# Loading the first rows of a in one transfer with a third row a head, in a fused state-space and feed-forward kernel

## The chip, the cores and the metric

The kernel runs on one core of a Trainium2 chip. A core has TensorE (PE, matrix products), VectorE (DVE), ScalarE (ACT), GpSimd (POOL) and SyncE (SP), which here only issues DMAs; each takes its own instructions in order, and semaphores tie them together. Data lie in SBUF and PSUM, both of 128 partitions, and come from DRAM by DMA over 16 DMA engines. The metric is the device time of one execution in microseconds, lower is better.

## The reference

Two blocks one after the other, all in float32. The first is a state-space scan over 4 batches and 8 heads of 768 steps, with inputs x (32 wide), B and C (16 wide) and a decay `a` per head and step:

```python
log_a = np.log(np.clip(a, 1e-06, 1.0))
for c in range(nc):                     # chunks
    cum = np.cumsum(la, axis=-1)
    L = np.exp(cum[:, :, :, None] - cum[:, :, None, :]) * causal
    y_intra = einsum('bhij,bhjd->bhid', einsum('bhin,bhjn->bhij', Cc, Bc) * L, xc)
    y_inter = einsum('bhin,bhnd->bhid', Cc, state) * np.exp(cum)[..., None]
    y[:, :, sl] = y_intra + y_inter
    state = decay_full * state + sum_j(Bc x_c * exp(cum_end - cum_j))
```

The second takes y as 3072 tokens of 256 and computes `g = h * sigmoid(1.702 h)` with `h = y @ w_in` (256 x 2048), and then `g @ w_out` (2048 x 256). The result does not depend on the chunk length; the kernel uses chunks of 64.

## The kernel before

**Tiling.** The 3072 tokens are six groups of 512 (`TG`). A group is two *pairs* of 256 steps, a pair is two blocks of 128, and a block is two chunks of 64. Batch 0 has 768 steps, so it is pairs 0, 1 and 2; pairs 0 and 1 make group 0, and pair 3 is the first of batch 1. For each group the state-space block gives `yT` (256 x 512, features on the partitions), `hidden` multiplies it with 16 tiles of w_in (`h`, two passes of 512 columns each, then Silu on ScalarE), and a second product goes through w_out. In later groups these products are done in a Strassen-like form (L934, L944, L1039).

**The order of work.** It is written out by hand, and `in_order` (L21) makes every engine follow the program text. So an instruction that waits holds back all that stands behind it on its engine. Hooks such as `at(in_hidden[0], k, ...)` put work behind the k-th tile of `hidden` of group 0.

**The start.** Everything that group 0 needs hangs on the first 512 steps of `a` of batch 0. They come in as `az0`, 128 x 256: four copies (one for each quarter of the partitions) of 32 rows, and in each copy row 2h + c holds half c of head h. Four DMAs load them, two from SP and two from ScalarE's queue (L278). Then: VectorE clips `az0` (L342), ScalarE takes the logarithm (L344), VectorE sums it up within chunks (`cum`, L346). TensorE fills PSUM banks with the causal mask (L530) and adds cum_i - cum_j for all heads of pairs 0 and 1 (`ab`, L536, picked out of the rows by the 0/1 operand `pick0`), ScalarE takes the exponential (L557): these are the decays L. `fold_ident(0)` (L336) builds an operand for later scans; it stands on VectorE ahead of the clip.

B and C of group 0 are loaded in blocks of 32 and transposed by VectorE (`turn_first`). C is then masked by head parity into `CT`, for pair 0 and for pair 1 by GpSimd (`mask_first`, L632). TensorE turns B back (L609), computes the scores `cb` of pair 0 (L664), then `rows` (the decay since the group's start, L515, exponential on ScalarE at L520 as `since`), then the scores of pair 1. VectorE multiplies scores and L (`weigh`, L675), TensorE computes the chunks' gains `A` (L695), ScalarE and VectorE sum them to states (L712, L717), and `finish` forms y from an `intra` (L818) and an `inter` part (L804). TensorE has fillers in between, products of ones that nobody reads: `keep_busy`, `pads` and `dense`.

**Pair 2.** Its rows of `a`, the last third of batch 0, are loaded apart, by GpSimd into `az1`, clipped by VectorE, and copied by ScalarE under a mask (`pick1`) into `X` (`pick_a`); TensorE spreads X over partitions by `fan` (L418), between the `intra` parts of pairs 0 and 1, and the decays of pair 2 are scanned from that much later.

**The weights.** They are float64 values handed over as pairs of 32-bit words, and the kernel makes float32 of them in ten pieces: 0 to 3 are two tiles of w_in each, 4 and 5 four tiles each, 6 to 9 are w_out. `fetch(i)` loads piece i with two DMAs from SP (L181); `fields` (L193, L196, VectorE) cuts out exponent and mantissa, `clamp` (L204, L205, ScalarE) moves the exponent, `rounded` (L209) and `join` (L223, L229, both VectorE) assemble the number in `w_in`. `narrow(i)` is rounded, join and the next piece's fields in an order that depends on i; for pieces 0 to 3 a join of all columns is two instructions, in two parts four smaller ones. The order about w_in's first pieces is:

```python
    fetch(1, held=nc.gpsimd)
    for i in range(2, 6):
        fetch(i)
...
    for i, k, c in ((2, 1, 1), (3, 2, 2), (4, 4, 7), (5, 8, 10), (6, 10, 14), (7, 14, 15)):
        at(in_hidden[0], k, lambda i=i: narrow(i))
        at(in_hidden[0], c, lambda i=i: clamp(i + 1))
```

`held` puts a memset by GpSimd (L172) ahead of piece 1's DMAs, into their target; it stands on GpSimd behind `since_start(0)` (`CsT`, L649), which needs `since`. SP, in order, therefore issues pieces 1 to 5 and all behind them only then. Other SP loads that come up: `az` (all of a), `spread_rows` (`af`, L272: rows of a read with each row repeated for 16 partitions), and `a<-scratch` (L262).

Of the kernel before, what the change touches and what calls it, by code (L numbers as in the profile page):

```python
# [16 lines left out]
P = 128  # L17
TG = 512
# [17 lines left out]
def kernel(  # L36
# [71 lines left out]
    az0 = ffn.tile([P, TG // 2], FP32, tag="b", name="az0").rearrange("p (c s) -> p c s", c=2)  # L108
    az1 = const.tile([P, NC - CG, P], FP32, name="az1")
    cum = const.tile([P, 2, P], FP32, name="cum")  # L110
# [104 lines left out]

    def join(i, parts=1):

        name, f, n = PIECES[i]
        n //= parts
        low, m, p2 = bits.pop(i)[1], mantissa.pop(i), power.pop(i)  # L220
        for k in range(parts):
            cols, fs = slice(k * n * DM, (k + 1) * n * DM), slice(f + k * n, f + (k + 1) * n)
            nc.vector.scalar_tensor_tensor(out=p2[:, cols], in0=low[:, cols], scalar=0x80000000,  # L223
                                           in1=p2[:, cols], op0=ALU.bitwise_and, op1=ALU.bitwise_or)
            if name == "in":
                dst, h = w_in[:, fs].rearrange("p f k e -> p (f k e)").unsqueeze(1), 1
            else:
                dst, h = w_out[:, :, fs].rearrange("p c f e -> p c (f e)"), 2
            nc.vector.scalar_tensor_tensor(  # L229
                out=dst, in0=m[:, cols].bitcast(FP32).rearrange("p (h e) -> p h e", h=h),  # L230
                scalar=2.0 ** -20, in1=p2[:, cols].bitcast(FP32).rearrange("p (h e) -> p h e", h=h),
                op0=ALU.mult, op1=ALU.mult)
        for n in NEXT.get(i, ()):
            fetch(n)

    def narrow(i):
        rounded(i)
        if i in (2, 4, 5, 6):
            join(i, 2 if i in (4, 5) else 1)
        if i == 6:  # L240
            decay_rows(0)
        if i + 1 < len(PIECES):
            fields(i + 1)
        if i not in (2, 4, 5, 6):
            join(i, 2 if i == 3 else 1)

# [29 lines left out]

    for r in range(R):
        (nc.sync, nc.scalar)[r % 2].dma_start(  # L278
            out=az0[32 * r:32 * r + 32].rearrange("p k s -> p (k s)"),
            in_=a[:2, :, :TG].rearrange("b h (c s) -> (b h) c s", c=PG))  # L280
    early = const.tile([P, 1], FP32, name="early")
# [29 lines left out]

    pick0 = picker("pick0", PG, PG, 1)

# [20 lines left out]
    def fold_ident(k, engine=nc.vector):  # L334
# [5 lines left out]

    fold_ident(0)
    nc.vector.tensor_scalar(out=az0, in0=az0, scalar1=1e-6, scalar2=1.0, op0=ALU.max,  # L342
# [4 lines left out]
        out=cum.rearrange("p k s -> p (k s)"), data0=carry.rearrange("p k s -> p (k s)"),  # L347
        data1=cum.rearrange("p k s -> p (k s)"), initial=0.0, op0=ALU.mult, op1=ALU.add)

    fans, flat = {}, {}  # L350
# [6 lines left out]

    def pick_a(p):

        assert divmod(2 * p, NC) == (0, CG)  # L360
        X = ffn.tile([P, 2, DM], FP32, tag="ob", name=f"X{p}")
        X = fans[p] = X.rearrange("p k (q i) -> p k q i", q=Q)
        for q in range(Q):
            nc.scalar.activation(X[:, :, q], az1, AF.Copy, scale=pick1[:, q:q + 1])


    APART = P // NH
    nc.gpsimd.memset(az1, 1.0)
    nc.gpsimd.dma_start(
        out=az1.rearrange("(h e) c s -> h e (c s)", e=APART)[:, 0], in_=a[0, :, TG:])  # L370

# [10 lines left out]
    for n in range(PG):  # L382
        t = whose[32 * n:32 * n + 32, n:n + 1]
        nc.gpsimd.affine_select(out=t, in_=t, pattern=[[-1, 1], [-PG, NH], [0, N]],
                                compare_op=ALU.is_equal, fill=0.0, base=-n,
                                channel_multiplier=1)
# [6 lines left out]
        out=part, in_=same[:, :, 0].rearrange("p (r q) -> p q r", q=Q), op=ALU.add, axis=AX.X)  # L393
    pick1 = const.tile([P, Q], FP32, name="pick1")
    nc.vector.tensor_reduce(
        out=pick1, in_=ident.rearrange("p (r q e) -> p q r e", q=Q, e=APART)[:, :, :, 0],
        op=ALU.add, axis=AX.X)

# [24 lines left out]
    def fan_all(p):  # L423

        ab = area(f"ab{p}")[:, :, :2 * Q * H]
        for r in range(R):
            fan(p, r, ab[:, r])
        fans[p] = ab

    def decay_fanned(p):  # L430
# [78 lines left out]
    def since_first():  # L509

        since[0] = ssd.tile([P, NC, P], FP32, tag="since", name="since0")
        rows = [bank(f"rows{p}")[:, :2 * P] for p in range(PG)]
        for p in range(PG):
            at = slice(32 * p, 32 * p + 32)
            nc.tensor.matmul(out=rows[p],  # L515
                             lhsT=whose[at, p].rearrange("p h n -> p (h n)"),
                             rhs=cum[at].rearrange("p k s -> p (k s)"), start=True, stop=True,
                             tile_position=(32 * p, 0), skip_group_check=True)
        for p in range(PG):
            nc.scalar.activation(since[0][:, 2 * p:2 * p + 2].rearrange("p c s -> p (c s)"),  # L520
                                 rows[p], AF.Exp)

    def drops():
# [42 lines left out]
    def area(name):  # L566
        return psa.tile([P, R, 4 * P], FP32, tag="cb", name=name)

    def turn_only(p, steps=range(3)):
# [14 lines left out]
        if 1 in steps:  # L584
            s["tp"] = s.pop("both")[:, 1]
            s["CT"] = ssd.tile([P, 2, Q, P], FP32, tag="CT", name=f"CT{p}")
            for q in range(Q):
                copy(s["CT"][:, :, q], s["tp"], part[:, q:q + 1])
        if 2 in steps and p < PG:
            tp = s["tp"]  # L590
            s["tp"] = ssd.tile([P, 2, P], FP32, tag="CsT", name=f"C{p}", bufs=3)
            copy(s["tp"], tp)
# [33 lines left out]
    def mask_first(p):  # L626

        s = st[p]
        s["CT"] = ssd.tile([P, 2, Q, P], FP32, tag="CT", name=f"CT{p}")
        if p:  # L630
            nc.vector.memset(s["CT"][:, 0, 0, :1], 0.0)
        nc.gpsimd.tensor_tensor(  # L632
# [137 lines left out]
    def finish(pairs, steps=range(2)):  # L770
# [39 lines left out]
        def intra(n, p):  # L810
            L = Ls[p]
            for k in range(2):
                for h in range(NH):
                    for i, side in enumerate(SIDES):
# [54 lines left out]
    def hidden(g, f):  # L869
# [3 lines left out]
        h = bank(f"h{g}_{f}")  # L873
        n = 2 if g == 0 and f in range(10, 13) else 1
        for k in range(NK):
# [277 lines left out]

    keep_busy(4, 0)
    both = area("ab0")
# [5 lines left out]
    turn_first("B")  # L1161
    clip(az1)
    differ_of(0)
# [5 lines left out]
    fields(0)  # L1169
    mask_first(1)  # L1170
    pick_a(PG)
    to = area("cb0")
    pads(9, to[:, 0])
    turn_back()
    ends_first(0)
    ends_first(1)
    rounded(0)
    score(range(PG), since_first, to)
    weigh(0)
# [260 lines left out]
```

## Time and profile before

| | us |
|---|---|
| three timed runs | 347.11, 347.58, 348.89 (median 347.58) |
| profiled execution, its own time | 347.67 |
| its span | 345.9 |
| TensorE busy | 339.2 (98%) |
| VectorE busy | 256.1 (74%) |
| ScalarE busy | 155.1 (45%) |
| GpSimd busy | 16.7 (5%) |

The profile is one execution. All times within it are counted from the start of the span; the span is a little shorter than the device time. A line such as `27.28 0.69 DVE p L193` reads: at 27.28 us, for 0.69 us, VectorE ran an instruction of line 193 that writes `p`. An `x96` behind it counts several instructions taken together, `SPq` is a DMA being issued on SP, `DMA` the transfer itself, `PEld` TensorE's loading of weights. The granted clock of TensorE is given in parts of full speed; it is full in every slice of this profile.

### The profile page before, as it was taken

The numbers are of one execution on the slowest core, as the hardware profiler recorded it, in microseconds if no ns is written. First come the engines' busy times: TensorE is split into PE (matmuls) and PEld (weight loads), VectorE is DVE, ScalarE is ACT, GpSimd is POOL, SyncE is SP. The second block draws the span as 40 slices with busy tenths as digits, with TensorE's granted clock in tenths as the row PEclk, the third lists the DMA queues.
The fourth block names the chain that finished last, engine by engine and source line by source line (L and its number), as shares of the span: only waits on it lengthen the run. The fifth ranks groups of instructions, "written<-read, shape, count | busy, mean of one in ns | idle before, by whom it ended". The sixth has DMA issues, their size and how long they took to land.

```text
span 345.9 us, 8116 instructions
## 1 busy us (share of the span) xinstructions
PE 339.2 (98%) x3380; PEld 270.2 (78%) x3380; DVE 256.1 (74%) x484; ACT 155.1 (45%) x352; POOL 16.7 (5%) x40
## 2 busy tenths in 40 slices
PE   8999999999999999999999999999999999999996
PEld 6633744555788888888888888888888888899996
DVE  5988999999799998858995667787564654465463
ACT  5786771507454324754332554442454322554320
POOL 7300110300000100000000000000000000000000
PEclk9999999999999999999999999999999999999999
DMA  6698899545637100435603036400000300000401
GB/s 160 132 289 211 217 239 133 152 67 102 122 63 127 36 0 15 65 99 100 110 27 51 2 78 121 64 0 3 0 4 2 62 2 0 0 2 0 63 0 62
DMA packets 90004, 25.76 MB, mean 74 GB/s; under 512 B 73416, under 2 KB 87248, under 8 KB 89968
## 3 DMA queue, kind: packets, MB, share of 16 engines
q1 hardware_dynamic: 89104, 24.72, 35.0%
q10 hardware_dynamic: 832, 0.52, 0.5%
q8 instruction: 26, 0.43, 0.5%
q14 instruction: 10, 0.08, 0.1%
q0 software_dynamic: 32, 0.01, 0.0%
HBM read 22.00 MB, written 3.24 MB: 73 GB/s over the span
## 4 chain that ended last, share of the span: by engine, by line
PE 92%; DMA 3%; SPq 2%; DVE 1%; issue 0%; ACT 0%; POOL 0%; DVEq 0%
PE acc L1039 28%; PE X L934 19%; PE Y L944 14%; PE o L976 8%; PE acc L1046 7%; PE h L878 7%; DMA bits<-in_moe_w_in_dram 3%; PE y L818 2%; PE cb L664 2%; SPq L181 1%; PE y L804 1%; PE A L695 1%; PE ab L536 1%; DMA az<-in_a_dram 1%; POOL CsT L649 0%
## 5 line engine op out<-in xcount | busy, mean ns | idle before, releaser
L939 ACT ACTIVATE ac<-X 128x256 f32<-128x256 f32 x76 | 29.1, 383 | 81.7 <-PE X L934 81.0
L1039 PE MATMUL acc<-mg,mw 128*128 128x256 f32 x192 | 54.5, 379 | 0.0
L1066 DVE TENSOR_TENSOR gT<-Y,ac 128x512 f32<-128x512 f32 x38 | 26.2, 689 | 38.1 <-PE Y L944 32.5
L911 ACT ACTIVATE gT<-gT 128x512 f32<-128x512 f32 (+1 forms) x76 | 38.9, 519 | 29.3 <-DVE gT L1066 28.8
L934 PE MATMUL X<-my,mi 128*128 128x256 f32 x152 | 45.2, 380 | 0.0
L1039 PEld LDWEIGHTS acc<-mg,mw 128*128 128x128 f32 x192 | 36.6, 190 | 4.9
L1066 DVE TENSOR_TENSOR gT<-Y,b 128x256 f32<-128x256 f32 x38 | 15.8, 419 | 28.5 <-PE Y L944 28.5
L878 PE MATMUL h<-yT,w_in 128*128 128x512 f32 (+1 forms) x92 | 35.5, 541 | 1.4 <-DVE w_in L229 0.9
L1039 PE MATMUL acc<-gT,w_out 128*128 128x256 f32 x128 | 35.5, 380 | 0.0
L878 PEld LDWEIGHTS h<-yT,w_in 128*128 128x128 f32 x92 | 17.2, 190 | 18.2 <-issue 12.8
L934 PEld LDWEIGHTS X<-my,mi 128*128 128x128 f32 x152 | 28.0, 190 | 4.0 <-ACT ac L939 0.3
L976 PE MATMUL o<-gT,w_out 128*128 128x512 f32 x64 | 28.3, 596 | 0.0
L902 DVE TENSOR_TENSOR mg<-gT 128x512 f32<-128x512 f32 x40 | 27.2, 681 | 0.0
L1039 PEld LDWEIGHTS acc<-gT,w_out 128*128 128x128 f32 x128 | 24.3, 190 | 3.4 <-ACT yT L853 0.2
L939 ACT ACTIVATE b<-X 128x256 f32<-128x256 f32 x38 | 14.6, 383 | 20.8 <-PE X L934 20.3
L934 PE MATMUL X<-yT,w_in 128*128 128x256 f32 x76 | 23.2, 389 | 0.0
L944 PE MATMUL Y<-yT,w_in 128*128 128x256 f32 x76 | 22.7, 381 | 0.0
L944 PE MATMUL Y<-my,mi 128*128 128x256 f32 x76 | 22.7, 381 | 0.0
L934 PE MATMUL X<-my,w_in 128*128 128x256 f32 x76 | 22.5, 380 | 0.0
L944 PE MATMUL Y<-yT,mi 128*128 128x256 f32 x76 | 22.5, 380 | 0.0
L976 PEld LDWEIGHTS o<-gT,w_out 128*128 128x128 f32 x64 | 11.9, 190 | 13.6 <-issue 12.7
L408 DVE TENSOR_TENSOR_SCAN L<-a,idents 128x1024 f32<-128x1024 f32 x9 | 20.5, 2279 | 0.3 <-DMA a<-scratch 0.3
(152 smaller groups left out, 547.8 us busy)
## 6 DMA issues: line engine op xcount, KB each, us to landing
a<-scratch SPq DMA_DIRECT2D x18, 256.0 KB, 4.9
bits<-in_moe_w_out_dram SPq DMA_DIRECT2D x8, 512.0 KB, 7.4
x<-in_x_dram SPq DMA_DIRECT2D x24, 128.0 KB, 3.7
out_dram<-ob SPq DMA_DIRECT2D x40, 64.0 KB, 2.0
bits<-in_moe_w_in_dram SPq DMA_DIRECT2D x8, 256.0 KB, 3.7
bits<-in_moe_w_in_dram SPq DMA_DIRECT2D x4, 512.0 KB, 11.4
b<-in_B_dram SPq DMA_DIRECT2D x20, 64.0 KB, 3.3
af<-in_a_dram SPq DMA_DIRECT2D x3, 384.0 KB
```

The costliest lines, as they stand in the source:

```text
L408: nc.vector.tensor_tensor_scan(out=L, data0=ra[p].rearrange("p k e -> p (k e)"), data1=idents.rearrange("p h i -> p (h i)"), initial=0.0, ...
L664: nc.tensor.matmul(out=s["cb"][side, r, k].rearrange("p (q i) -> p q i", q=Q), lhsT=BT[rows, k, side], rhs=CT[rows, k, :, side], start=Tru ...
L878: nc.tensor.matmul(out=h[:, cols], lhsT=w_in[:, f, k], rhs=yT[g][:, k, cols], start=(k == 0 and c == 0), stop=(k == NK - 1), skip_group_ch ...
L902: nc.vector.tensor_tensor(out=t[:, 0:2], in0=B[:, :, 1], in1=B[:, 0], op=ALU.subtract)
L911: nc.scalar.activation(o, i, AF.Silu, scale=GELU_SCALE)
L934: nc.tensor.matmul(out=s["X"], lhsT=lhsT, rhs=rhs, start=i == "1", stop=i == "4", skip_group_check=True)
L939: nc.scalar.activation(copy, s["X"], AF.Copy)
L944: nc.tensor.matmul(out=o, lhsT=lhsT, rhs=rhs, start=s.pop("new", False), stop=i != "5", skip_group_check=True)
L976: nc.tensor.matmul(out=o[c], lhsT=w_out[:, c, f], rhs=gT[g, f // 2][:, f % 2], start=(f == 0), stop=(f == NF - 1), skip_group_check=True)
L1039: nc.tensor.matmul(out=acc[g][0][i][:, cols], lhsT=w, rhs=h[:, cols], start=(j == 0 and k == 0 and (i, 0) in begins), stop=(j == NF // 2 - ...
L1046: nc.tensor.matmul(out=o[k] if type(o) is list else o[:, cols], lhsT=h[:, cols], rhs=w, start=(j == 0 and (i, k) in begins), stop=(j == NF ...
L1066: nc.vector.tensor_tensor(out=o, in0=v, in1=w, op=ALU.add)
```

## The change

`az0` now holds, in each of its four copies, 32 rows that run through the array as it lies: row 3h + c is the c-th 256 steps of head h, so that pair 2's rows (c = 2) are there too. One DMA on SP loads it, its source read four times over. `pick0` and `whose` step by 3 rows a head (NR), and `third` takes pick1's place. Beyond that:

- `az1`, its memset, its DMA on GpSimd and its clip go; `pick_a` makes X from the clipped `az0` with two multiplications and a memset on VectorE.
- CT of pair 1 is masked by ScalarE (`mask_blocks`), not by GpSimd.
- `fold_ident(0)` stands behind the scan to `cum`, `fold_ident(1)` in `narrow(6)`.
- Fillers: `keep_busy` 3 for 4, `pads` 6 for 9, `dense` 4 blocks of 64 columns for 8, into the free half of a `rows` bank.
- `intra` of group 0 runs by heads, then blocks, rather than by blocks, then heads.
- Joins: piece 1 in two parts; the first half of piece 3 ahead of piece 4's `fields`, the second behind; `clamp(4)` one tile later; tile 9 of `hidden` in two passes of half the columns for each weight.
- `turn_only` copies C's transpose out of PSUM for pair 3 as well (its condition was p < 2, which no call met).

```diff
-    def join(i, parts=1):
+    def join(i, parts=1, only=None):
...
-        for k in range(parts):
+        for k in range(parts) if only is None else only:
...
     def narrow(i):
         rounded(i)
         if i in (2, 4, 5, 6):
+            if i == 6:
+                fold_ident(1)
             join(i, 2 if i in (4, 5) else 1)
         if i == 6:
             decay_rows(0)
+        if i == 3:
+            join(i, 2, (0,))
         if i + 1 < len(PIECES):
             fields(i + 1)
-        if i not in (2, 4, 5, 6):
-            join(i, 2 if i == 3 else 1)
+        if i == 3:
+            join(i, 2, (1,))
+        elif i not in (2, 4, 5, 6):
+            join(i)
...
-    for r in range(R):
-        (nc.sync, nc.scalar)[r % 2].dma_start(
-            out=az0[32 * r:32 * r + 32].rearrange("p k s -> p (k s)"),
-            in_=a[:2, :, :TG].rearrange("b h (c s) -> (b h) c s", c=PG))
+    NR = S // (2 * P)
+    assert NH * NR <= 32 <= BH * NR
+    nc.sync.dma_start(
+        out=az0.rearrange("p k s -> p (k s)"),
+        in_=a.rearrange("b h (c s) -> (b h c) s", c=NR)[:32].unsqueeze(0).to_broadcast(
+            [R, 32, 2 * P]))
...
-    pick0 = picker("pick0", PG, PG, 1)
+    pick0 = picker("pick0", PG, NR, 1)
...
-    fold_ident(0)
     nc.vector.tensor_scalar(out=az0, in0=az0, scalar1=1e-6, scalar2=1.0, op0=ALU.max,
                             op1=ALU.min)
...
+    fold_ident(0)
...
-    def pick_a(p):
-
-        assert divmod(2 * p, NC) == (0, CG)
-        X = ffn.tile([P, 2, DM], FP32, tag="ob", name=f"X{p}")
-        X = fans[p] = X.rearrange("p k (q i) -> p k q i", q=Q)
+    def pick_a():
+
+        X = ffn.tile([P, 2, DM], FP32, tag="ob", name="X")
+        X = fans[PG] = X.rearrange("p k (q i) -> p k q i", q=Q)
         for q in range(Q):
-            nc.scalar.activation(X[:, :, q], az1, AF.Copy, scale=pick1[:, q:q + 1])
-
-
-    APART = P // NH
-    nc.gpsimd.memset(az1, 1.0)
-    nc.gpsimd.dma_start(
-        out=az1.rearrange("(h e) c s -> h e (c s)", e=APART)[:, 0], in_=a[0, :, TG:])
+            nc.vector.tensor_scalar(out=X[:, :, q], in0=az0, scalar1=third[:, q:q + 1],
+                                    scalar2=None, op0=ALU.mult)
+        nc.vector.memset(X.rearrange("p k q (s i) -> p k q s i", s=2)[:, :, :, :, 0], 0.0)
...
-    pick1 = const.tile([P, Q], FP32, name="pick1")
-    nc.vector.tensor_reduce(
-        out=pick1, in_=ident.rearrange("p (r q e) -> p q r e", q=Q, e=APART)[:, :, :, 0],
-        op=ALU.add, axis=AX.X)
+    third = const.tile([P, Q], FP32, name="third")
+    for q in range(Q):
+        at = NR * q + PG
+        nc.vector.tensor_reduce(
+            out=third[:, q:q + 1], in_=ident[:, at:at + 3 * (32 + NR * Q) + 1:32 + NR * Q],
+            op=ALU.add, axis=AX.X)
...
-        if 2 in steps and p < PG:
+        if 2 in steps and p == PG + 1:
             tp = s["tp"]
             s["tp"] = ssd.tile([P, 2, P], FP32, tag="CsT", name=f"C{p}", bufs=3)
             copy(s["tp"], tp)
...
         s["CT"] = ssd.tile([P, 2, Q, P], FP32, tag="CT", name=f"CT{p}")
-        if p:
-            nc.vector.memset(s["CT"][:, 0, 0, :1], 0.0)
         nc.gpsimd.tensor_tensor(
...
         def intra(n, p):
             L = Ls[p]
-            for k in range(2):
-                for h in range(NH):
+            for h, k in [(h, k) for h in range(NH) for k in range(2)] if early else [
+                    (h, k) for k in range(2) for h in range(NH)]:
                     for i, side in enumerate(SIDES):
...
-        n = 2 if g == 0 and f in range(10, 13) else 1
+        n = 2 if g == 0 and f in range(9, 13) else 1
...
-    keep_busy(4, 0)
+    keep_busy(3, 0)
...
     turn_first("C")
     turn_first("B")
-    clip(az1)
+    pick_a()
     differ_of(0)
...
     fields(0)
-    mask_first(1)
-    pick_a(PG)
+    mask_blocks(1)
     to = area("cb0")
-    pads(9, to[:, 0])
+    pads(6, to[:, 0])
     turn_back()
     ends_first(0)
     ends_first(1)
     rounded(0)
-    score(range(PG), since_first, to)
+    free = []
+    score(range(PG), lambda: free.append(since_first()), to)
...
-    dense(8, bank("dense"))
+    dense(4, free[0])
     finish(range(PG))
     join(0, 2)
-    fold_ident(1)
     fields(1)
     clamp(1)
     table(AF.Silu)
     rounded(1)
-    join(1)
+    join(1, 2)
     fields(2)
...
-    for i, k, c in ((2, 1, 1), (3, 2, 2), (4, 4, 7), (5, 8, 10), (6, 10, 14), (7, 14, 15)):
+    for i, k, c in ((2, 1, 1), (3, 2, 3), (4, 4, 7), (5, 8, 10), (6, 10, 14), (7, 14, 15)):
         at(in_hidden[0], k, lambda i=i: narrow(i))
         at(in_hidden[0], c, lambda i=i: clamp(i + 1))
```

More of the change, by code (lines that the diff above doesn't have):

```diff
@@ L108 @@
     az0 = ffn.tile([P, TG // 2], FP32, tag="b", name="az0").rearrange("p (c s) -> p c s", c=2)
-    az1 = const.tile([P, NC - CG, P], FP32, name="az1")
     cum = const.tile([P, 2, P], FP32, name="cum")
@@ L214 @@
     NEXT = {1: (6,), 5: (9,)}
-    def join(i, parts=1):
+    def join(i, parts=1, only=None):
         name, f, n = PIECES[i]
         n //= parts
-        low, m, p2 = bits.pop(i)[1], mantissa.pop(i), power.pop(i)
-        for k in range(parts):
+        low, m, p2 = bits[i][1], mantissa[i], power[i]
+        for k in range(parts) if only is None else only:
             cols, fs = slice(k * n * DM, (k + 1) * n * DM), slice(f + k * n, f + (k + 1) * n)
@@ L232, in join @@
                 op0=ALU.mult, op1=ALU.mult)
-        for n in NEXT.get(i, ()):
-            fetch(n)
+        if only is None or parts - 1 in only:
+            for t in bits, mantissa, power:
+                t.pop(i)
+            for n in NEXT.get(i, ()):
+                fetch(n)
     def narrow(i):
@@ L356, in clip @@
         nc.vector.memset(t.rearrange(by_chunk, s=2)[:, :, :, 0], 0.0)
-    def pick_a(p):
-        assert divmod(2 * p, NC) == (0, CG)
-        X = ffn.tile([P, 2, DM], FP32, tag="ob", name=f"X{p}")
-        X = fans[p] = X.rearrange("p k (q i) -> p k q i", q=Q)
-        for q in range(Q):
-            nc.scalar.activation(X[:, :, q], az1, AF.Copy, scale=pick1[:, q:q + 1])
-    APART = P // NH
-    nc.gpsimd.memset(az1, 1.0)
-    nc.gpsimd.dma_start(
-        out=az1.rearrange("(h e) c s -> h e (c s)", e=APART)[:, 0], in_=a[0, :, TG:])
+    assert divmod(2 * PG, NC) == (0, CG) and NC - CG == 2
+    assert DM == Q * P
+    def pick_a():
+        X = ffn.tile([P, 2, DM], FP32, tag="ob", name="X")
+        X = fans[PG] = X.rearrange("p k (q i) -> p k q i", q=Q)
+        for q in range(Q):
+            nc.vector.tensor_scalar(out=X[:, :, q], in0=az0, scalar1=third[:, q:q + 1],
+                                    scalar2=None, op0=ALU.mult)
+        nc.vector.memset(X.rearrange("p k q (s i) -> p k q s i", s=2)[:, :, :, :, 0], 0.0)
     same = ssd.tile([P, NH, D], FP32, tag="BT", name="same")
@@ L383 @@
         t = whose[32 * n:32 * n + 32, n:n + 1]
-        nc.gpsimd.affine_select(out=t, in_=t, pattern=[[-1, 1], [-PG, NH], [0, N]],
+        nc.gpsimd.affine_select(out=t, in_=t, pattern=[[-1, 1], [-NR, NH], [0, N]],
                                 compare_op=ALU.is_equal, fill=0.0, base=-n,
@@ L423, in fan_all @@
     def fan_all(p):
-        ab = area(f"ab{p}")[:, :, :2 * Q * H]
+        whole = area(f"ab{p}")
+        ab = whole[:, :, :2 * Q * H]
         for r in range(R):
@@ L428, in fan_all @@
         fans[p] = ab
+        return whole
     def decay_fanned(p):
@@ L511, in since_first @@
         since[0] = ssd.tile([P, NC, P], FP32, tag="since", name="since0")
-        rows = [bank(f"rows{p}")[:, :2 * P] for p in range(PG)]
+        whole = [bank(f"rows{p}") for p in range(PG)]
+        rows = [t[:, :2 * P] for t in whole]
         for p in range(PG):
@@ L521, in since_first @@
                                  rows[p], AF.Exp)
+        return whole[0][:, 2 * P:]
     def drops():
```

## The prediction

> **What bounds the kernel now.** I read the page first: engines, slices, issues.
>
> ```profile
> span 345.9 us, 8116 instructions
> ## 1 busy us (share of the span) xinstructions
> PE 339.2 (98%) x3380; PEld 270.2 (78%) x3380; DVE 256.1 (74%) x484; ACT 155.1 (45%) x352; POOL 16.7 (5%) x40
> ...
> af<-in_a_dram SPq DMA_DIRECT2D x3, 384.0 KB
> ```
>
> TensorE is busy nearly always, so time can be won or lost only where it waits. The list of TensorE's waits names its last one at 29.5 us: everything behind that follows without a pause, so a shift of TensorE at about 33 us reaches the end unchanged. (The last line is used further down: `af` is the one load without a landing time.) Then the chain of waits, for the first 30 us (start, duration, what ran):
>
> ```profile
> 1.59 2.30 DMA az<-in_a_dram
> ...
> 5.66 2.67 PE ab L536 x96
> ...
> 11.15 1.02 POOL CsT L649
> 12.17 0.05 POOL bits L172
> ...
> 17.15 9.61 DMA bits<-in_moe_w_in_dram
> ...
> 27.28 0.69 DVE p L193
> ```
>
> The first load of a lands at 1.59 + 2.30 = 3.89. From it come `cum`, the decay matmuls, `rows`, `since`, `CsT`, and the little memset of L172 that holds back the fetch of w_in pieces 1 to 5. Piece 4 is usable at 27.28; VectorE, in order, stands before it and only then joins piece 3. Three lines of the timeline show SP's issue of a and TensorE's last two waits near the start (time, duration, instruction; in brackets what it waited before and for whom):
>
> ```profile
> 0.81 1.58 SPq L278 DMA_DIRECT2D az<-in_a_dram  x2
> ```
>
> ```profile
> 11.08 0.70 PE L664 MATMUL cb<-CT,Bt 32*64 32x128 f32 x32 [0.43 <-POOL CT L632]
> ```
>
> ```profile
> 29.52 3.67 PE L878 MATMUL h<-yT,w_in 128*128 128x512 f32 x8 [0.85 <-DVE w_in L229]
> ```
>
> The last is the wait for piece 3, so a's landing sets everything up to 29.5 us. Last, three stretches (length; busy time of PE, PEld, DVE, ACT, POOL; granted clock, DMA share, GB/s):
>
> ```profile
> 43.00:44.00 1.00, 1.00 (x4) 0.50 (x3) 0.99 (x1) 1.00 (x3) 0.00 (x0) 1.00 1.10 368
> 155.20:156.20 1.00, 1.00 (x6) 0.90 (x5) 0.63 (x2) 0.34 (x1) 0.00 (x0) 1.00 0.62 157
> 4.00:5.50 1.50, 1.36 (x9) 0.84 (x7) 1.00 (x2) 1.01 (x2) 1.43 (x3) 1.00 0.93 241
> ```
>
> Weights keep all 16 DMA engines busy (1.10, 368 GB/s). In 155.2 to 156.2 nearly all that moves is the load of `af`, and 0.62 is reached, little more than half.
>
> **The change part by part.** The sum is made against the profiled run's own time, 347.67 us (span 345.9 and 1.77 around it), 0.09 above the median of 347.58.
>
> 1. *One load of a.* Two issues go from SP (1.58) and two from ACT; one of 128 KB at 0.81 comes. C's loads on ACT's queue move from 2.23 to about 0.9, SP's B, w_in and x loads up by 0.8. The question is how many engines carry it. `af` reads with an outermost dimension of 8 on the DRAM side (128 partitions in SBUF) and gets little more than half of the 16's time. The new load's DRAM side begins with a repeat of 4, so I take it to use 4. At 241/16 = 15 to 368/16 = 23 GB/s per engine, 128 KB on four take 1.4 to 2.1 us, where 32 KB on sixteen take 0.1. The 32 KB loads land 2.1 to 2.4 after issue, so alone the new one lands at 0.81 + 2.3 + 1.3..2.0 = 4.4 to 5.1. C's 256 KB now move beside it, 16 KB on each engine, 0.7 to 1.0 us if all of it goes first: 4.4 to 6.1. With sixteen engines and no collision the floor is 0.81 + 2.4 = 3.2. I take 5.2, the middle of the four-engine bounds: 1.3 later; ends 0.7 earlier (3.2) and 2.2 later (6.1). The Trainium skill, "DMA: Bandwidth & Descriptors", section "Why a DMA increments its semaphore by 16 and not by 1", has it that a DMA goes to the largest number of engines up to 16 that divides the outermost dimension of both sides; by that the number here is 4, and `af`'s 0.62 agrees for 8.
>
> 2. *VectorE's head.* fold_ident(0) goes from ahead of the clip to behind the scan. Before, the clip still had 0.20 us of idle ahead of it, so it hid nothing; now 0.6 us (its pitch) lies between scan and transposes, with another reduce (0.08), and C's transpose starts about 0.9 later than its 6.68. B's transpose ends near 9.5, before its bank is free (ACT L557 ended 8.70, now 10.0): covered by the decay matmuls. If a lands at 3.2, that cover shrinks and the fold costs up to 0.3.
>
> 3. *POOL.* az1's memset and DMA (3.26 to 4.61) and C's second mask (1.04) go. `same` is ready 1.35 earlier, for nobody: VectorE is still waiting for a. Of the mask, TensorE's 0.43 us wait at 11.08 is the price, and goes. ScalarE does two 128x256 masks where it did two copies into X (0.93 us): nothing.
>
> 4. *X on VectorE.* Two 0.42 us multiplies (pitch 0.34) and a memset replace a clip of 0.54 and two memsets: +0.1, hidden, since weigh waits for the score, not for VectorE. Had the score been early, 0.1 on the path.
>
> 5. *Fillers and orders on TensorE.* keep_busy loses 0.64, pads 0.12, dense 0.5 us, all beside waits. intra's new order issues the same 64 passes in 0.93 us; if two on the same 32 columns could not overlap it would be up to twice that, 0.9 for each of two pairs. I take 0, as the state they feed comes later anyway; with 1.8 hidden(0) starts later, but step 7 shows 0.8 of slack there.
>
> 6. *Gate of the fetch and start of hidden(0).* rows, since and CsT keep their distance to a: L172 and SP's issue at 12.23 go to 13.5, piece 4 from 27.28 to 28.58. SP stays blocked in L181 (1.90) as now: the x loads ahead of it moved no more than 0.8. The score's second half starts right behind rows, +1.3 - 0.43 = +0.87, and hidden(0) at 17.89 + 0.9 less 0.2 for the shorter dense = 18.6. fold_ident(1) (0.6) leaves VectorE's path there and lands ahead of join(6), in an idle 0.53 before L223 at 42.76 (0.1 left, with join(6) due 1.6 later). Piece 1 in two halves costs four 0.42 for two 0.69 (+0.2) and frees f=2 0.6 earlier.
>
> 7. *Half of piece 3 joined ahead of fields(4).* f=6 no longer waits for piece 4. Before, TensorE started f=8 at 29.52 + 2 x 1.72 = 32.96, which is 5.68 behind piece 4. Now, behind piece 4, VectorE has fields(4) 1.21, the second half of join(3) 0.80, rounded(4) 1.13, the first half of join(4) 1.41: 4.55, and 0.07 to TensorE: 4.62. f=8 starts at 28.58 + 4.62 = 33.20. TensorE itself would be there at 18.6 + 8 x 1.72 = 32.4, so VectorE binds, with 0.8 to spare. ScalarE's clamp(4), now behind h=3's Silu, keeps its place as that matmul is long done. Two passes of 256 columns for f=9: 0.
>
> 8. *tp of pair 3 copied on ScalarE* (0.36) frees a bank 2 us earlier; ScalarE idles 3.62 there. 0 to +0.
>
> Sum: 1.3 later from a, 1.06 earlier (5.68 - 4.62) from the join: f=8 0.24 later, 347.67 + 0.2 = **347.9 us**. With a at 4.4 to 6.1: 347.1 to 348.8.
>
> **The rivals.**
>
> *Sixteen engines.* The load uses all, a lands at 3.2 to 3.9, fold and filler fit, and piece 4 comes up to 0.7 earlier. For it: a-scratch's loads repeat rows too and have a normal landing (4.9). Against: their outermost repeat is 64, not 4, and `af`. f=8 at 26.6 + 4.62 = 31.2 to 31.9: 345.9 to 346.6. If besides SP's 1.90 us issue does not recur, piece 4 stops binding and TensorE arrives itself, at 16.6 + 13.8 + 0.3 = 30.7: 345.4.
>
> *TensorE falls back to its slow pace.* The first passes of 128x192 are 0.32 apart and the mask's eight of 128x256 take 1.43 us, the first ones at half the rate of the last: TensorE begins slow and quickens at about 4.6. With keep_busy shorter, its work before a ends near 4.9 and a's matmuls start at 5.66 + 1.3 = 6.96: a gap of 2.1 us, where the longest now, 0.85, was followed by full pace. If it falls back, the 5.4 us of matmuls between `ab` and the scores run at half pace for 3 to 5 us: +1.5 to 2.5 on the gate, 349.4 to 350.4, slower. It decides once that chain loses 1.5 us. Against it: the clock column stays at 1.00 in every stretch. The Trainium skill, "TensorE: Matmul & The Clock Gate", Part 1, has the gate close after about 3.4 us idle, so by it 2.1 us would leave it open and the time at 347.9; no run here shows a gap of that length.
>
> **How the numbers follow.** A measurement of this kernel can tell about 0.5%, 1.74 us: faster is under 345.84, slower over 349.32. Forecast: 0.39, own range 347.1 to 348.8, all within. Sixteen engines: 0.27, 0.20 of it under 345.84 when SP's stall goes too or a has no collision. Slow pace (or four engines still slower, a after 6.7, same sign): 0.34. Hence faster 0.20, same 0.46, slower 0.34. The range leaves a tenth at each side: 345.6 to 349.9.
>
> **What would show it.** az landing near 5.2 (with four engines, no landing time or a low DMA share around 3 to 5 us); VectorE's clip waiting some 2 us for it; `ab` at about 7.0; SP's L180 at 13.5; no wait of f=6, a wait of 0.5 to 0.9 us of f=8 for w_in. A clip before 4.0 makes me wrong towards faster; `ab` over 3.5 us for its 96 matmuls, towards slower.

## The result and the profile after

The changed kernel takes 352.42 us (median of six runs, 350.66 to 353.10), the kernel before 347.37 in the same comparison: 1.0133 times as long, 95% interval 1.0103 to 1.0164. The forecast was 347.9 and the range ended at 349.9. The profiled execution took 350.66, the shortest of the six. In every ratio of this document, executions more than 1.5% above the fastest of their kernel are left out. The page of the changed kernel begins:

```profile
span 348.7 us, 8106 instructions
## 1 busy us (share of the span) xinstructions
PE 340.8 (98%) x3376; PEld 271.5 (78%) x3376; DVE 255.9 (73%) x487; ACT 155.1 (44%) x353; POOL 13.9 (4%) x37
```

TensorE is busy for 1.6 us more than before, though it has slightly less to do. The chain of waits (start, duration, what ran) says where:

```profile
0.80 5.07 DMA az<-in_a_dram
...
5.89 0.30 DVE az L351
...
7.42 4.12 PE ab L551 x96
...
20.69 14.12 PE h L891 x32
```

The load of a lands at 5.87, not 3.89. And the 96 matmuls of `ab`, 2.67 us before, take 4.12. SP, GpSimd and the weights have left the chain: from 20.69 on TensorE itself is what everything waits for. One line of the list of waits (total, times, longest) and two of TensorE's timeline show the pause ahead of `ab` and its pace:

```profile
PE ab L551 <- DVE cum L355: 2.2, 1, 2.2
```

```profile
7.42 1.16 PE L551 MATMUL ab<-cum,pick 32*64 32x128 f32 x32 [2.21 <-DVE cum L355]
...
10.76 0.73 PE L551 MATMUL ab<-minus,cum 32*128 32x128 f32 x16
```

The first 32 matmuls take 1.16 us where they took 0.69; the last 16 take 0.73 as before. So behind the pause TensorE runs at half pace and quickens at 10.8. It had run at half pace ahead of the pause too: the mask's eight products, the same in both kernels, take longer now. First the kernel before, then the changed one:

```profile
3.94 1.43 PE L530 MATMUL ab<-below,identb 128*128 128x256 bf16 x8
```

```profile
3.29 1.91 PE L545 MATMUL ab<-below,identb 128*128 128x256 bf16 x8
```

Before, the last of them come at twice the rate of the first. Now all eight are 0.21 us apart, as the first ones were, and TensorE goes into the pause at 5.2 without having quickened at all. So the pause did not slow it down here: TensorE came out of it as slow as it went in.

A stretch of the same trace (columns as in the prediction, the last two are the share of the 16 DMA engines and GB/s), in which a is still moving on SP's queue (q1) and the rest of C on ScalarE's (q10), and the shares of the two queues:

```profile
5.00:5.80 0.80, 0.20 (x1) 0.00 (x0) 0.00 (x0) 0.00 (x0) 0.69 (x3) 1.00 0.27 90
```

```profile
q1 hardware_dynamic: 49, 0.04, 15.2%
q10 hardware_dynamic: 39, 0.03, 12.1%
```

0.27 of sixteen is four engines, and a does not even have them to itself.

A ledger of the kernels that follow, all from their profiled executions: start of `hidden`, start of the first product with w_out (`o`), and the end of the span.

| | hidden | o | hidden to o | span | time |
|---|---|---|---|---|---|
| before | 17.89 | 47.23 | 29.34 | 345.9 | 347.67 |
| changed | 20.69 | 49.22 | 28.53 | 348.7 | 350.66 |
| changed, once more | 23.64 | 52.18 | 28.53 | 351.1 | 353.11 |
| load in four | 18.23 | 46.75 | 28.53 | 345.8 | 347.72 |
| before with the one load | 22.53 | 50.57 | 28.04 | 349.4 | 351.10 |
| TensorE kept busy | 19.35 | 47.88 | 28.53 | 347.2 | 349.20 |

The changed kernel loses 2.80 us up to `hidden`, gains 0.81 there (before had waited 0.85 for piece 3), and loses 0.8 behind `o`. Rows two and three are executions of one program 2.45 us apart, and ahead of `hidden` they are already 2.95 apart.

### The profile page after: what moved, and what is told of

Same layout as the page of the kernel before. It is cut to its first block, busy times and chain, and to the rows that moved or that the text cites. A ratio compares the mean times of both kernels' runs of the same rounds, so it can differ in the third digit from the quotient of the medians.

```text
span 348.7 us, 8106 instructions
## 1 busy us (share of the span) xinstructions
PE 340.8 (98%) x3376; PEld 271.5 (78%) x3376; DVE 255.9 (73%) x487; ACT 155.1 (44%) x353; POOL 13.9 (4%) x37
## 4 chain that ended last, share of the span: by engine, by line
PE 96%; DMA 1%; ACT 1%; DVE 0%; issue 0%
PE acc L1052 28%; PE X L947 19%; PE Y L957 14%; PE h L891 10%; PE o L989 8%; PE acc L1059 7%; PE y L831 3%; PE cb L677 2%; PE y L817 1%; DMA az<-in_a_dram 1%; PE A L708 1%; PE ab L551 1%; PE tp L594 0%; DVE cum L355 0%; ACT yT L851 0%
## 5 line engine op out<-in xcount | busy, mean ns | idle before, releaser
L891 PEld LDWEIGHTS h<-yT,w_in 128*128 128x128 f32 x96 | 17.9, 190 | 16.6 <-issue 12.2
## 6 DMA issues: line engine op xcount, KB each, us to landing
bits<-in_moe_w_in_dram SPq DMA_DIRECT2D x4, 512.0 KB, 10.8
```

Of the source, the lines that this page charges most:

```text
L891: nc.tensor.matmul(out=h[:, cols], lhsT=w_in[:, f, k], rhs=yT[g][:, k, cols], start=(k == 0 and c == 0), stop=(k == NK - 1), skip_group_ch ...
```

## The experiments

**The changed kernel once more.** No edit.

> The changed kernel, unaltered, timed and profiled once more beside the next three. Theory: the load of a goes over few DMA engines and lands late (5.87 us in the profile, 3.89 before), and in the pause before it (2.21 us) TensorE falls to a slower pace, so that the 96 matmuls of ab take 4.12 us instead of 2.67. The profiled execution lost 2.8 us up to the first matmul of hidden and its time was 350.66, while the median of six was 352.42. If the slow pace lasts longer in most executions, a second profile near 352.4 shows the ab matmuls, or those right behind them, 1.5 us longer than 4.12. Rival: the further 1.8 us lie behind 50 us, and the start is the same to 0.3 us.

352.24 us, ratio 1.0103 (1.0038 to 1.0169); the profile is of an execution of 353.11. Its timeline of TensorE:

```profile
7.57 1.16 PE L551 MATMUL ab<-cum,pick 32*64 32x128 f32 x32 [2.36 <-DVE cum L355]
...
10.91 1.24 PE L551 MATMUL ab<-minus,cum 32*128 32x128 f32 x16
...
15.89 1.16 PE L677 MATMUL cb<-CT,Bt 32*64 32x128 f32 x32
...
20.53 0.69 PE L429 MATMUL ab<-X,ones 32*64 32x256 f32 x16
```

Here half pace lasts behind the pause from 7.57 to about 20.3, through `ab`, the scores (1.16 for 0.69) and the gains; ahead of it the mask takes 1.91 us again, so TensorE had not quickened in this execution either. That is more than the 1.5 us of the theory: `hidden` starts 2.95 later than in the first profile. Yet the stretch in the middle of it shows the full clock:

```profile
8.90:12.30 3.40, 3.40 (x76) 2.62 (x76) 2.69 (x7) 1.16 (x2) 1.04 (x1) 1.00 1.17 198
```

So the clock column's 1.00 does not rule out half pace.

**Four loads instead of one.**

```diff
-    nc.sync.dma_start(
-        out=az0.rearrange("p k s -> p (k s)"),
-        in_=a.rearrange("b h (c s) -> (b h c) s", c=NR)[:32].unsqueeze(0).to_broadcast(
-            [R, 32, 2 * P]))
+    for r in range(R):
+        (nc.sync, nc.scalar)[r % 2].dma_start(
+            out=az0[32 * r:32 * r + 32].rearrange("p k s -> p (k s)"),
+            in_=a.rearrange("b h (c s) -> (b h c) s", c=NR)[:32])
```

> The changed kernel with a loaded by four transfers of 32 partitions each, two from SP and two from ScalarE's queue as before, in the new layout of three rows a head; all else as changed. Theory (late load and slow pace are the whole loss): a lands at 3.9, ab takes 2.7 us again, hidden starts at 17.5 to 18.1 and the time is 346.3 to 347.4, no slower than before. Rival (the reordered joins, X on VectorE, the fold behind the scan or the new order of intra cost as much): at least 349. Rival for the slow ab matmuls (the new layout of rows, not the pause): ab takes about 4.1 us here too.

347.35 us, ratio 0.9999 (0.9971 to 1.0027). a lands at 3.31 and the pause is gone. TensorE comes to `ab` as slow as in the changed kernel (the mask takes 1.91 us here too), but it works on without a pause and has full pace 0.3 us into `ab`:

```profile
5.21 0.88 PE L551 MATMUL ab<-cum,pick 32*64 32x128 f32 x32
6.02 0.73 PE L551 MATMUL ab<-minus,cum 32*128 32x128 f32 x16
```

With the same layout, X, masks, joins, fillers and orders as the changed kernel, the loss is gone. So it needs the one load, and with a quick load everything else in the change is worth nothing that can be measured, neither way.

**The one load in the kernel before.** The three-row load, with `pick0` and `whose` to match, and nothing else.

```diff
-    for r in range(R):
-        (nc.sync, nc.scalar)[r % 2].dma_start(
-            out=az0[32 * r:32 * r + 32].rearrange("p k s -> p (k s)"),
-            in_=a[:2, :, :TG].rearrange("b h (c s) -> (b h) c s", c=PG))
+    nc.sync.dma_start(
+        out=az0.rearrange("p k s -> p (k s)"),
+        in_=a.rearrange("b h (c s) -> (b h c) s", c=NR)[:32].unsqueeze(0).to_broadcast(
+            [R, 32, 2 * P]))
...
```

> The kernel before with nothing changed but the load: one transfer in the layout of three rows a head (pick0 and whose follow), pair 2's rows still loaded apart. Theory: a lands near 5.9, TensorE waits about 2.0 us, ab takes 4.1 us; the gate of the weights' fetch moves by 3.4, piece 4 from 27.28 to 30.7, and since the order of the joins is the old one all of it reaches the end: 347.4 + 3.4 = 350.8 us. Rival (the pause does not slow TensorE when keep_busy is as long as before): a's 2.0 alone, 349.4. Rival (the load costs nothing that lasts): under 348.5.

351.30 us, ratio 1.0109 (1.0075 to 1.0144). The load alone brings the loss, at about the price expected (350.8), though by another way: TensorE comes out of the pause at full pace (the first 32 of `ab` take 0.69), and it is slowed in the middle of `ab`. This trace does record it. Five stretches of it, the granted clock is third from the end:

```profile
5.50:8.80 3.30, 1.76 (x61) 1.17 (x66) 2.72 (x6) 1.94 (x4) 2.34 (x6) 1.00 0.55 168
8.90:12.30 3.40, 3.40 (x78) 2.39 (x70) 1.58 (x6) 2.54 (x7) 1.64 (x2) 0.52 1.11 167
12.30:15.70 3.40, 3.40 (x89) 2.09 (x97) 1.42 (x4) 1.54 (x4) 0.77 (x3) 0.50 0.03 4
15.70:19.10 3.40, 3.40 (x104) 1.73 (x92) 3.40 (x3) 2.76 (x5) 0.94 (x2) 0.50 0.37 108
19.20:22.00 2.80, 2.80 (x176) 2.11 (x162) 2.73 (x8) 1.09 (x3) 0.00 (x0) 0.99 0.91 264
```

The pause is 1.54 us, ahead of 7.34. Some 1.6 us after TensorE has resumed the clock falls to 0.50, and it stays there for 10.2 us although TensorE is busy all the time. A mean clock of 0.985 over the span, which five more of the ten executions show, is just that: 10.2 x 0.5 / 349 = 1.5%. The Trainium skill, "TensorE: Matmul & The Clock Gate", Part 1, describes a gate that judges TensorE in free-running windows of 3.41 us and halves its clock; 10.2 us is three of those windows, and the scatter from execution to execution fits a window that does not begin with the kernel. That a pause must be as long as a window, as the prediction drew from that page, does not hold here: 1.54 us were enough. One other trace shows the clock fall behind a pause, that with the DMA engines to itself (below): 1.52 us, and a clock of 0.50 from 8.4 on. In the changed kernel's two it had not risen yet.

**TensorE kept busy until a is there.**

```diff
     for r in range(R):
+        if r == R - 1:
+            keep_busy(6, 0)
         mask_banks(1, r, bank(f"ab1_{r}"))
```

> The changed kernel with six more filler products (128x192, keep_busy's) ahead of the last mask, so that TensorE is busy until about 7 us and the pause before a's matmuls falls from 2.2 to some 0.4 us. Theory (the pause slows it): ab takes 2.7 instead of 4.1 us and hidden starts 1.4 us earlier, 20.69 to 19.3; the time falls by 1.0 to 1.4, or by more if the executions of 352.4 have a longer slow stretch: 349 to 351. Rival (something else slows ab): ab still 4.1 us and no change from the changed kernel, 352.4.

Ratio 1.0111 (1.0028 to 1.0195), over executions of 349.20, 350.54 and 351.22; a fourth took 354.54 at a mean clock of 0.990, as some 7 us at half pace would give (an estimate: 7 x 0.5 / 353 = 1%). In the profile, that of 349.20, a is as late as ever and `ab` at full pace:

```profile
7.31 0.70 PE L551 MATMUL ab<-cum,pick 32*64 32x128 f32 x32 [0.30 <-DVE cum L355]
...
9.22 0.73 PE L551 MATMUL ab<-minus,cum 32*128 32x128 f32 x16
```

`hidden` starts at 19.35, 1.34 earlier than in the changed kernel's first profile, and the time is 1.46 shorter. So with the pause filled `ab` is quick, though the load is as late and the layout the same. By the spacing of its matmuls TensorE had quickened at 4.4 in this execution, still in the mask and ahead of the added fillers; it stayed quick. The other executions are not explained by this profile, and by the ratio alone the fillers do not clearly help.

**The same, and a full product for the small pads.** Of `pads(6, ...)`, tiles of 32 x 32, became two products of 128 x 256.

```diff
-    pads(6, to[:, 0])
+    dense(4, to[:, 0])
+    dense(4, to[:, 1])
```

> The changed kernel with six more keep_busy products ahead of the last mask, as in the run before, and with two products over the whole array (128x256) in place of the six small pads. In the slow stretches the matmuls are half as fast for 3.4 us or three times that, as if decided once every 3.41 us by how full the array was. Theory: with the pauses filled, no stretch is judged idle; hidden starts at 19.1 to 19.4, the time is 348.6 to 349.6 and the runs lie within 1.5 us. Rival (the pads were enough, or the loss of the other executions lies elsewhere): median 350.9 and a spread of over 2 us again.

349.33 us, ratio 1.0045 (1.0021 to 1.0068), ten executions within 2.0 us (expected: 1.5), all at a mean clock of 0.999 or 1.000. `hidden` starts at 20.06, later than expected, since the fillers themselves now run until 7.9 and 11.4. More than half of the changed kernel's loss is gone, with a still landing at 6. The rest, 0.45% or 1.6 us, is the late load with the fillers that run beyond it; the two were not told apart.

**The load with the DMA engines to itself.** B, C, piece 0 and x are held back until a is clipped (the memset is in `load_first`, on the target).

```diff
+        nc.vector.memset(t[:, 0, :1], 0.0)
...
-    load_first("C", [nc.scalar] * R)
-    load_first("B", [nc.sync] * R)
-    fetch(0)
-    load(0, "x")
-    load(1, "x")
...
     nc.vector.tensor_scalar(out=az0, in0=az0, scalar1=1e-6, scalar2=1.0, op0=ALU.max,
                             op1=ALU.min)
+    load_first("C", [nc.sync] * R)
+    load_first("B", [nc.sync] * R)
+    fetch(0)
+    load(0, "x")
+    load(1, "x")
```

> The changed kernel with the loads of B, C, piece 0 and x held back until a is clipped (VectorE's memset into their targets stands behind the clip), so that the one transfer of a has the DMA engines to itself; the time is not compared, only a's landing is looked at. Theory: four of sixteen engines carry it, at some 22 GB/s each, and B and C in front of and among it make up the rest of the delay: 128 KB alone take about 1.5 us where 32 KB on sixteen took 0.1, so a lands 1.4 later than a quick load, at 4.4 to 4.9, with a DMA share near 0.25 while it runs. Rival (the collision is everything): 3.2 to 3.5. Rival (the few engines are everything): 5.6 or later, as before.

VectorE can clip at 5.12, with a DMA share of 0.27 while a moves. One line of the timeline, and one stretch:

```profile
5.12 0.29 DVE L347 TENSOR_SCALAR az<-az 128x256 f32<-128x256 f32 x1 [1.91 <-DMA az<-in_a_dram]
```

```profile
3.50:4.50 1.00, 1.00 (x6) 0.73 (x5) 0.00 (x0) 0.00 (x0) 0.86 (x3) 1.00 0.27 97
```

0.2 later than expected, and between the rivals: of 2.4 us from four quick loads (clip at 3.51) to the one (5.89), 1.6 are there with the few engines alone, and 0.8 come with the company of B and C.

**Two loads of two copies each.**

```diff
-    nc.sync.dma_start(
-        out=az0.rearrange("p k s -> p (k s)"),
-        in_=a.rearrange("b h (c s) -> (b h c) s", c=NR)[:32].unsqueeze(0).to_broadcast(
-            [R, 32, 2 * P]))
+    for i, queue in enumerate((nc.sync, nc.scalar)):
+        queue.dma_start(
+            out=az0[64 * i:64 * i + 64].rearrange("p k s -> p (k s)"),
+            in_=a.rearrange("b h (c s) -> (b h c) s", c=NR)[:32].unsqueeze(0).to_broadcast(
+                [2, 32, 2 * P]))
```

> The changed kernel with a loaded in two transfers of 64 partitions, one from SP and one from ScalarE's queue ahead of C, each reading its 32 rows twice (outermost dimension 2, not 4); only a's landing is looked at. Theory (the outermost dimension sets the number of engines, and both take the same ones): two engines carry 128 KB, share near 0.13, a lands at 7 to 9 us. If each takes two others: four engines as before, 5.5 to 6. Rival (the engines do not depend on that dimension, and the size of a transfer counts): 64 KB each land earlier than 5.87, at 4 to 5.

```profile
6.82 0.29 DVE L352 TENSOR_SCALAR az<-az 128x256 f32<-128x256 f32 x1 [3.60 <-DMA az<-in_a_dram]
```

```profile
5.00:6.00 1.00, 0.20 (x1) 0.00 (x0) 0.00 (x0) 0.00 (x0) 0.80 (x3) 1.00 0.13 45
```

Half the bytes per transfer, two queues, and a comes later, a little before the 7 us expected: two engines of sixteen (0.13) at 22 GB/s each. Outermost 4 gave 0.27, outermost 2 gives 0.13. In this stretch SP's transfer moves nearly alone. That both use the same two engines is inferred from the landing, which the expectation put at 5.5 to 6 for four. By the rule of the Trainium skill, "DMA: Bandwidth & Descriptors", section "Why a DMA increments its semaphore by 16 and not by 1", the counts are 4 and 2; the trace agrees.

**A quick load and a late VectorE.** Four loads as above, and

```diff
+    for _ in range(4):
+        fold_ident(0)
     nc.vector.tensor_scalar(out=az0, in0=az0, scalar1=1e-6, scalar2=1.0, op0=ALU.max,
                             op1=ALU.min)
```

> The kernel with four quick loads of a, and VectorE held up ahead of the clip by four more fold_ident (2.4 us), so that a is there at 3.3 but its sums come when they come in the changed kernel. Theory (only the time of a's sums and the pause of TensorE matter, not the transfer): as the changed kernel, 351 to 353, with runs spread over 3 us. Rival (the few-engine transfer itself slows what runs beside it, such as B, C or the weights): 348 to 350.

353.54 us, ratio 1.0157 (1.0092 to 1.0221). The pause before `ab` is 2.59 us, and half pace lasts until about 20.7:

```profile
7.79 1.16 PE L553 MATMUL ab<-cum,pick 32*64 32x128 f32 x32 [2.59 <-DVE cum L357]
```

So beyond its lateness no cost of the load shows: 2.4 us of VectorE ahead of `cum` cost as much. Here too the mask takes 1.9 us, and TensorE had not quickened ahead of the pause.

**Piece 3 joined in the old order**, on top of four loads.

```diff
-        if i == 3:
-            join(i, 2, (0,))
...
-            join(i, 2, (1,))
+            join(i, 2)
...
-    for i, k, c in ((2, 1, 1), (3, 2, 3), (4, 4, 7), (5, 8, 10), (6, 10, 14), (7, 14, 15)):
+    for i, k, c in ((2, 1, 1), (3, 2, 2), (4, 4, 7), (5, 8, 10), (6, 10, 14), (7, 14, 15)):
```

> The changed kernel with four quick loads of a, and piece 3 joined as before: fields(4) first, then both halves of join(3), and clamp(4) behind tile 2. By the prediction's step 7 the first half ahead of fields(4) is worth 1.06 us where VectorE waits for piece 4. Theory now: VectorE did not wait for piece 4 in the profile with four loads (it was busy up to 27.8, and piece 4 landed at 26.9), so f=8's weights are joined at 32.3 as well; f=6 waits 0.7 to 0.9 us for its half, and the time is within 0.2% of the kernel with four loads. Rival (step 7 as predicted): 0.3% slower.

347.11 us, ratio 1.0006 (0.9983 to 1.0028): no worth of the half join can be measured. Not even the expected wait of f=6 shows: VectorE comes to piece 4 without a wait, so it was there well ahead of the 26.9 us that the expectation had taken from the trace with four loads.

```profile
25.81 0.69 DVE L192 TENSOR_SCALAR p<-bits 128x1024 uint32<-128x1024 uint32 x1
```

`hidden` to `o` is 28.16 us, 0.37 less than with the half join, where TensorE waits 0.12 to 0.13 us ahead of f=8 in every trace.

**Three attempts at a faster kernel**, all with four loads. The first puts one full product in the place of the six pads.

```diff
-    pads(6, to[:, 0])
+    dense(4, to[:, 0])
```

> The changed kernel with four quick loads of a, and one product over the whole array (128x256) in place of the six small pads. The kernel with four loads alone ran 346.2 to 349.1, median 347.35, ratio 0.9999. Theory (part of that spread is a stretch of 3.4 us at half pace, let in by the small pads): median 346.3 to 346.9, runs within 1.5 us, 0.2 to 0.4% below the kernel before. Rival (the spread has other causes): as before, within 0.2%.

348.97 us, ratio 1.0051 (1.0036 to 1.0066): slower, and both theories missed. `hidden` starts at 17.43, the earliest so far, but far behind it TensorE stands without an instruction to run:

```profile
149.93 0.78 PE L831 MATMUL y<-L,x 64*32 64x64 f32 x54 [1.02 <-issue]
```

The second also loads pair 1's x from ScalarE's queue (behind the table load for Exp), and takes intra's old order.

```diff
-    load(1, "x")
...
     table(AF.Exp)
+    load(1, "x", nc.scalar)
```

> As best1, with pair 1's x loaded from ScalarE's queue behind the table load for Exp instead of last on SP's queue, and intra of group 0 in the old order. In the profile with four quick loads, the last x lands at 12.04 and TensorE's gains A wait 0.6 us for it, and VectorE's sum of the steps, the joins and tile f=8 follow; the new order of intra takes 1.22 us where the old one takes 0.93. Theory: A starts at 10.9 and does not wait, hidden starts 0.7 to 0.9 earlier, at 17.3 to 17.6, f=8 0.4 to 0.8 earlier; 345.6 to 346.4 us. Rival (the conversion of the weights binds, f=8 stays at 32.3): as best1.

352.53 us, ratio 1.0157 (1.0129 to 1.0184). x comes later, not earlier (12.43 for the waiting matmuls of `A`), and behind it TensorE waits 1.55 us for instructions at 16.0; half of the six executions then show a mean clock of 0.985 to 0.989. Theory and rival both fell. Two things were altered at once and not taken apart, so the cause stays open. The third is the first, with five pads ahead of the first filler, so that TensorE has as many instructions as with the six pads.

```diff
-    keep_busy(3, 0)
+    keep_busy(3, 5)
```

> The kernel with four quick loads and one full product in place of six pads, with five small pads put ahead of keep_busy, so that TensorE has as many instructions as with the six pads. Without them it ran 348.97, 0.5% slower than before, though hidden started 0.8 us earlier: the profile shows TensorE without instructions (a wait named issue) for 1.02 us at 148.9, in a burst of small matmuls, just behind a 16 KB packet of the instruction queue, and 0.37 at 82.8. Theory (where these fetches fall among the bursts depends on the count of instructions ahead): the waits behind 47 us go back to 0.4 or less, and the time to 346.3 to 347.4, ratio 0.997 to 1.000. Rival (the full product itself, or a stretch at half pace, costs): again 348.5 to 349.5.

347.22 us, ratio 0.9996 (0.9975 to 1.0016). The time is back where it was expected, and the wait at 149 is gone. The profiled execution, the slowest of the twelve at 348.28, waits 1.2 us in all at 82 to 84 instead, partly for a load of x, so the waits did not vanish as expected; that the place of the fetches is the whole cause of the 0.5% is likely, not shown. No version beats the kernel before by what can be measured.

## Why the prediction was wrong

The step that failed is in the sum itself: it ran the matmuls behind the pause at full pace. It counts that a comes later, and nothing for the pace of what follows the pause. The runs showed half pace there instead: up to 10.8 us in one profiled execution of the changed kernel and up to 20.3 in the other, where `hidden` starts 1.34 and 4.29 us behind the profile with the pause filled (19.35).

*Step 1* held in its mechanism: four engines, at 22 GB/s each. Alone a would come at 5.1, the end of the estimate of 4.4 to 5.1; with B and C it came at 5.87, inside 4.4 to 6.1 but 0.7 above the value taken. Against the transfers before it is 2.0 later, not 1.3. SP's loads of weights and x did not move up by 0.8 but back by 1.7 (piece 0 from 4.50 to 6.24), since SP's fourth load of B waited until a had landed; TensorE had no wait for them in this trace.

*The rival of the slow pace is what came true*, and was given 0.34. Its place (`ab`) and its first price were right: +1.45 in the first profile. Its pause was right as a number, 2.21 for 2.1, partly by luck: TensorE's work ended 0.3 later than forecast, at 5.2, and `ab` started 0.46 later. Three things in it were wrong. TensorE did not fall back in the changed kernel's two profiles: it had not quickened yet. The time of 4.6 was read from one execution and is not fixed: it is 4.4 in the profile with six more fillers, whose start is the same, 5.5 with four loads, and in these two it did not come by 5.2. The clock fell in the kernel before with the one load. The evidence against the rival, "the clock column stays at 1.00 in every stretch", is none: the same column reads 1.00 in a stretch where every matmul takes twice its time, and it read 1.00 over the slow first fillers that the prediction itself had described. And the stretch was sized at 3 to 5 us, where the second profile has 12.7 behind the pause. The other five executions of the first six took 351.87 to 353.10 us, most of them nearer to it than to the first, and two show a mean clock of 0.985, as 10 us at half pace give. Hence, most likely, 352.4 and not 349.4 to 350.4. *Step 5* had costed the shorter fillers at nothing because they stood beside waits. Their shortening shows no cost of its own: with the one load, the kernel before, with its longer fillers, loses as much (1.0109, and 1.0103 for the changed kernel in the same comparison). What counted was the pause. Six more fillers in it did not clearly bring the time down alone (1.0111); with full products for the pads as well, more than half the loss went (1.0045).

*Step 6* had the gate keep its distance to a. Its issue came at 15.15, 2.92 later, not 1.3: a's 2.0 and `ab`'s 1.45, less the wait for the mask (0.43), add up to 3.0. *Step 3*'s wait went, as forecast. Of *step 5*, intra in the new order costs 0.29 for pair 0 (1.22 for 0.93); 0 was taken, 0.9 was the bound.

*Step 7* counted 4.55 us from piece 4's `fields` to f=8's weights; measured are 30.23 to 34.78, 4.55. But the credit of 1.06 supposed that VectorE waits for piece 4, and it no longer did: 30.23 follows the half join without a gap. Nor does it in the old order, with four loads (25.81, above) or in the kernel before with the one load, where `hidden` to `o` took 28.04. So the 0.81 us that the changed kernel gains there cannot be put down to the half join: without it, and without that wait, the stretch is shorter still (28.16 and 28.04). The sum thus had one term too small (a, by 0.7), one that did not count (the join, 1.06), and lacked the largest (half pace, 1.3 to 4.3).

## What to carry to other kernels

A load that repeats a few rows should put its copies into separate transfers: the outermost dimension, not the size, set how many of the 16 DMA engines worked. (A large dimension outermost in one transfer was not tried.) When a change makes TensorE wait in a stretch that everything hangs on, price not only the wait but the matmuls behind it at half pace for 3.4 and for 10 us, and see whether TensorE has reached full pace before the wait. Look for the pace in the matmuls' own durations, since the clock column may say nothing. Before the rest of a change is costed, see which engine binds after the shift, not before.

## What was not expected of the hardware

- Where the clock had risen, a pause of 1.54 us brought it down for 10.2 us, and one of 1.52 for some 13.5 (with a further pause of 2.94 in them). Where it had not, pauses of 2.2 to 2.6 us were followed by 3.3 us at half pace (10.8 less 7.4) in one execution and by nearly 13 in two others; during the long stretches TensorE was busy throughout, mostly with small tiles. What ends them was not tried apart: with more fillers, and full products in place of small ones, the runs lay closer together, 348.3 to 350.3, but the same exchange did not help with four loads.
- SP's fourth load of B was issued at 5.89, just when a had landed, though SP had nothing else to do from 2.95. The list of SP's waits puts it down to a's load; the trace has both loads on one semaphore. So a late load also held up those queued behind it:

```profile
SPq L134 <- DMA az<-in_a_dram: 2.9, 1, 2.9
```

- Five small products more or less at the start of TensorE's program moved the time by 0.5% (1.0051 and 0.9996), with its waits in other places.
